# Opening of an attention and SwiGLU kernel: order of transposes, scores, sums and casts

## Chip, core and metric

The kernel runs on one core of one Trainium2 chip. The metric is the device time of one execution in microseconds (us). The engines are TensorE (PE; its weight loads are listed as PEld), VectorE (DVE), ScalarE (ACT), GpSimd (POOL) and SyncE (SP), which only issues transfers here.

## What is computed

Causal attention with a window of 64 positions, for 8 batches and 8 heads of 576 positions with 64 values each, and then a SwiGLU block on the 4608 rows of 512 values that come out of it.

```python
scores = q @ k.T / sqrt(64)
mask = (rel >= 0) & (rel < 64)        # rel = row - column
attn = softmax(where(mask, scores, -1e9))
x = (attn @ v).transpose(0, 2, 1, 3).reshape(4608, 512)
g = x @ w_gate
out = (g * sigmoid(g) * (x @ w_val)) @ w_out     # d_ff = 1536
```

## The kernel before

The rows are worked on in nine tiles of 512 (`t` = 0 to 8). A tile is one batch's first 512 positions, except for tile 7, which holds the last 64 positions of all batches. Within a tile `u` = 0 to 3 counts pairs of heads. The order of instructions on each engine is the order in which the program issues them (a manual schedule); waits between engines come from the tiles and their buffers.

For each pair, `scores` (L200) multiplies keys and queries block by block into `s_ps`, a pair of PSUM banks, and ACT takes the exponential into `E`. Tile 0 has its mask as a bias that is added in PSUM by four matmuls with the identity (L227); later tiles multiply with a mask on DVE. `sums` (L242) adds up the weights with a matmul against ones (`d_ps`), and ACT forms the inverse as a logarithm (L251) and an exponential of its negative (L253). `values` (L257) multiplies weights and values into `ao_ps`, and DVE multiplies by the inverse into `xT` (L269). `gate_value` (L294) makes one of 12 steps `m` of the gate: four matmuls into `g_ps`, four into `v_ps`, then Silu on ACT and a product on DVE (`gate_end`). `project` (L331) has 12 chunks per output block of 128 rows.

Tile 0 is the opening. Its q and k come as float32 over SP and ACT, are cast by ACT, DVE and POOL (`casts`, L402), and turned by PE transposes into `tp` (L173), from which DVE or ACT copies q (L410) and DVE copies k (`split_k`, L176). The loop at L403 does this for one pair, then its scores. `keep_warm` (L358) issues matmuls whose result nobody reads. v of batch 0 comes as float32 over SP, is cast by POOL (`cast_v`, L146), and a copy shifted by half a block is made by DVE (`shift_v`, L150). For `values` all four blocks of both copies are needed.

The weights come over POOL's queue, which casts them: gate and value weights in column blocks of 256 (`weights_gv`, L158), then q of batch 1 (`load_qk`), then the output weights in three blocks (`weights_o`, L164), then v of batch 1. A ring allows eight of POOL's transfers to be open; the ninth waits for the first to land. The first two gate steps are built up pair by pair (`gate_part`, L275) between the values of the pairs.

The keys of batch 1 are loaded by ACT in steps m = 0 to 3, and in m = 4 to 7 each pair is cast by ACT, transposed by PE and copied by DVE within the same step (L456 to L461). From m = 8 on DVE turns the queries of batch 1 (`turn_q`). Then come the scores of tile 1 with halves of tile 0's projection between them (L467 to L470).

PSUM has two pools with two buffers per name: `ps_a` holds wide pairs of banks (scores, sums, values, and `tp` of batch 1), `ps_f` single banks under "g" and "v" (gate, projection, sums, `tp` of batch 0, warm-up).

Of the kernel before, what the change touches and what calls it, by code (L numbers as in the profile page):

```python
# [8 lines left out]
P = 128  # L9
FP32 = mybir.dt.float32  # L10
BF16 = mybir.dt.bfloat16
AF = mybir.ActivationFunctionType
# [5 lines left out]
def kernel(  # L18
# [127 lines left out]
    def cast_v(t, which=range(4)):  # L146
        for i in which:
            nc.gpsimd.tensor_copy(v1[t % 2][:, i], staged[t, "v"][:, i])  # L148

    def shift_v(t, copy, lo=0, hi=4):  # L150

        a, b = v1[t % 2], v2[t % 2]
        top = min(hi, 3)
        if top > lo:
            copy(b[64:128, lo + 1:top + 1], a[64:128, lo:top])
        copy(b[0:64, lo:hi], a[0:64, lo:hi])

    def weights_gv(f0, f1):  # L158
        for src, dst in ((moe_w_gate, wg), (moe_w_val, wv)):
            nc.gpsimd.dma_start(  # L160
                dst[:, :, f0:f1], src[:, f0:f1].rearrange("(c r) f -> r c f", r=P)
            )

    def weights_o(c0, c1):  # L164
        nc.gpsimd.dma_start(
            wo[:, c0:c1, :],
            moe_w_out[P * c0:P * c1].rearrange("(c r) f -> r c f", r=P),
        )
# [31 lines left out]
    def scores(t, u):  # L200

        qT = queries[t][:, u, :]
        E = epool.tile([P, 2, 512], BF16, name="E", tag="E")
        s_ps = ps_a.tile([P, 2, 512], FP32, name="s_ps", tag="a")
        if t == LAST:
            pieces = [
                (c, b, b + 1, kT[t % 2 if b < 4 else 2], P * (b % 4) + 64 * c)
                for b in range(8) for c in range(2)
            ]
        else:  # L210
            pieces = [(1, 0, 1, None, 0)] + [
                (j % 2, j, min(8, j + 2), kT[t % 2], 64 * j) for j in range(8)
            ]
        for i, (c, lo, hi, src, x) in enumerate(pieces):
            for h in range(2):
                r = slice(64 * h, 64 * h + 64)
                nc.tensor.matmul(  # L217
                    blocks(s_ps[64 * c:64 * c + 64, h], t, lo, hi),
                    zero[r] if src is None else src[r, u, x:x + 64],
                    blocks(qT[r], t, lo, hi),  # L220
                    start=t >= TURNED or i < 2, stop=t >= TURNED,
                )
        if t < TURNED:
            for c in range(2):
                for h in range(2):
                    r = slice(64 * h, 64 * h + 64)
                    nc.tensor.matmul(  # L227
                        s_ps[64 * c:64 * c + 64, h], identb[r, r],
                        bias[r, c ^ h].rearrange("r e i c x -> r (e i c x)"),
                        start=False, stop=True,  # L230
                    )
        nc.scalar.activation(E[:], s_ps[:], AF.Exp, scale=0.125)  # L232
        if t >= TURNED:
            nc.vector.tensor_mul(  # L234
                E[:].rearrange("r h x -> r (h x)"),
                E[:].rearrange("r h x -> r (h x)"),
                maskl[:].rearrange("r h e b x -> r (h e b x)") if t == LAST
                else mask[:].rearrange("r h e i c x -> r (h e i c x)"),
            )
        weights[t, u] = E  # L240

    def sums(t, us, d_ps, apart=False):  # L242

        for i, u in enumerate(us):
            for h in range(2):
                nc.tensor.matmul(  # L246
                    d_ps[64 * h:64 * h + 64, i], ones[:, 0:D], weights[t, u][:, h, :]
                )
        n = len(us)
        r = fsb.tile([P, 2, 512], FP32, name="r", tag="r", bufs=4)  # L250
        nc.scalar.activation(r[:, 0:n], d_ps[:], AF.Ln)  # L251
        for x in [r[:, i:i + 1] for i in range(n)] if apart else [r[:, 0:n]]:
            nc.scalar.activation(x, x, AF.Exp, scale=-1.0)  # L253
        for i, u in enumerate(us):
            inverse[t, u] = r[:, i]

    def values(t, u, o_ps):  # L257
        E = weights.pop((t, u))
# [10 lines left out]
        nc.vector.tensor_mul(xT[t][:, u, :], o_ps[:], inverse.pop((t, u)))  # L269

    def products(t, u):
        sums(t, (u,), ps_f.tile([P, 1, 512], FP32, name="d_ps", tag="v"))
        values(t, u, ps_a.tile([P, 2, 512], FP32, name="ao_ps", tag="a")[:, 0])

    def gate_part(t, ms, tiles, c):  # L275
        for m, pair in zip(ms, tiles):
            for ps, w in zip(pair, (wg, wv)):
                nc.tensor.matmul(  # L278
                    ps[:], w[:, c, P * m:P * m + P], xT[t][:, c, :],
                    start=(c == 0), stop=(c == 3),  # L280
                )
# [76 lines left out]
    def keep_warm(n):  # L358
        for _ in range(n):
            nc.tensor.matmul(warm[0:D], ones[:, 0:D], ones[:])  # L360

    keep_warm(8)
    nc.gpsimd.memset(tri[:], 1.0)
    for a in range(2):
        half = tri[64 * a:64 * a + 64]
# [30 lines left out]
    def wide(name):  # L396
        return ps_a.tile([P, 2, 512], FP32, name=name, tag="a")

    def join(copy, dst, src):
        copy(dst.rearrange("r e (h d) -> r h e d", h=2), src)  # L400

    casts = ((on_a, on_v), (on_p, on_v), (on_p, on_p), (on_p, on_p))  # L402
    for u in range(4):  # L403
        hs = slice(2 * u, 2 * u + 2)
        tps = []
        for i in range(2):
            join(casts[u][i], first[:, i, u], raw[i][:, hs])
            tps.append(ps_f.tile([P, 512], BF16, name="tp", tag="gv"[i]))
            transposes(tps[i], first[:, i, u])
        (on_v if u else on_a)(queries[0][:, u, :], tps[0][:])  # L410
        split_k(kT[0][:, u, :], tps[1][:])
        keep_warm(1)
        if u == 3:
            sums(0, (0, 1), wide("d_ps"))
        scores(0, u)
    weights_gv(0, 256)
    for i in range(0, 4, 2):
        cast_v(0, (i, i + 1))
        shift_v(0, on_v, i, i + 2)
    weights_gv(256, 512)  # L420
    weights_gv(512, 768)
    for f in range(768, DFF, 256):
        weights_gv(f, f + 256)
    load_qk(1)
    weights_o(0, 4)
    weights_o(4, 8)
    weights_o(8, 12)
    load_v(nc.gpsimd, v1[1], 1)
    keep_warm(4)
    sums(0, (2, 3), wide("d_ps"), apart=True)  # L430
    keep_warm(4)
    pairs = [gate_tiles() for _ in range(2)]
    for u in range(0, 4, 2):
        o_ps = wide("ao_ps")
        for i in range(2):
            values(0, u + i, o_ps[:, i])
        for c in range(u, u + 2):
            gate_part(0, (0, 1), pairs, c)
    set_silu()
    raw_k = stage.tile([P, H, 4, D], FP32, name="k_f", tag="k")  # L440
    for m in range(12):
        if m < 2:
            gate_end(0, m, pairs[m])
        else:
            gate_value(0, m)
        if m == 2:
            for i in range(4):
                nc.vector.tensor_copy(
                    mask[:, 0, :, i], tri[:].rearrange("r c (x e) -> r e c x", e=16)
                )  # L450
            nc.vector.memset(mask[64:128, 0, :, 0, 0, :], 0.0)
            nc.vector.tensor_copy(mask[:, 1], mask[:, 0])
        if m < 4:
            hs = slice(2 * m, 2 * m + 2)
            load_runs(nc.scalar, raw_k[:, hs], k, 1, hs)
        elif m < 8:  # L456
            u = m - 4
            tp = ps_a.tile([P, 512], BF16, name="tp", tag="a")
            join(on_a, keys[:, u], raw_k[:, 2 * u:2 * u + 2])
            transposes(tp, keys[:, u])  # L460
            split_k(kT[1][:, u, :], tp[:])  # L461
        if m >= 8:
            turn_q(1, m - 8)
# [12 lines left out]
        shift_v(1, on_v, i, i + 1)  # L476

    def d_tile():
        return ps_f.tile([P, 1, 512], FP32, name="d_ps", tag="v")

    for u in range(2):
        sums(1, (u,), d_tile())
    project(0, 2)
    for u in range(4):
        if u > 1:
            sums(1, (u,), d_tile())
        values(1, u, wide("ao_ps")[:, 0])
    project(0, 3)

    for t in range(1, NT):  # L490
# [68 lines left out]
```

## Time and profile before

| | |
|---|---|
| Median of three runs | 340.98 us (340.88 to 341.24) |
| Profiled run | 342.31 us, of which the span covers 340.4 |
| Granted TensorE clock, mean | 0.997 |
| First matmul of the gate's step m=2 | 24.54 us |
| First projection matmul of tile 0 | 46.78 us |
| First gate matmul of tile 1 | 61.10 us |

A line of the profile's timeline gives start, duration, engine, source line, operation, and what it writes and reads; `x4` means four instructions merged, and the bracket at its end the idle time of the engine before it and what ended it. A line of the waits gives who waited for whom, the total, how often, and the longest. In the page's 40 slices a digit is the busy share in tenths. The rates of a DMA view count bytes as they arrive, so a transfer that casts float32 to bfloat16 reads twice as many.

### The profile page before, as it was taken

The numbers are of one execution on the slowest core, as the hardware profiler recorded it, in microseconds if no ns is written. First come the engines' busy times: TensorE is split into PE (matmuls) and PEld (weight loads), VectorE is DVE, ScalarE is ACT, GpSimd is POOL, SyncE is SP. The second block draws the span as 40 slices with busy tenths as digits, with TensorE's granted clock in tenths as the row PEclk, the third lists the DMA queues.
The fourth block names the chain that finished last, engine by engine and source line by source line (L and its number), as shares of the span: only waits on it lengthen the run. The fifth ranks groups of instructions, "written<-read, shape, count | busy, mean of one in ns | idle before, by whom it ended". The sixth has DMA issues, their size and how long they took to land.

```text
span 340.4 us, 6984 instructions
## 1 busy us (share of the span) xinstructions
PE 327.5 (96%) x2732; PEld 154.3 (45%) x2732; DVE 214.8 (63%) x318; ACT 167.8 (49%) x237; POOL 140.2 (41%) x252
## 2 busy tenths in 40 slices
PE   8777899999999999999999999999999999999994
PEld 3443344444544444444444444454445444454441
DVE  5545568378766775696578657865777576754431
ACT  3654466435653566346534753376337633673310
POOL 4963536846756976206521997065200000000000
PEclk9999999999999999999999999999999999999998
DMA  8999999999699679809960999499501220020013
GB/s 261 207 180 239 213 188 225 136 210 196 116 228 228 73 120 235 178 4 160 212 155 2 138 181 184 31 135 210 134 0 33 75 73 2 16 79 32 3 31 92
DMA packets 84113, 44.38 MB, mean 130 GB/s; under 512 B 63856, under 2 KB 78704, under 8 KB 84080
## 3 DMA queue, kind: packets, MB, share of 16 engines
q0 software_dynamic: 48304, 22.30, 53.2%
q1 hardware_dynamic: 33760, 19.54, 21.1%
q10 hardware_dynamic: 2016, 2.10, 2.2%
q8 instruction: 21, 0.34, 0.4%
q14 instruction: 12, 0.10, 0.1%
HBM read 54.00 MB, written 9.44 MB: 186 GB/s over the span
## 4 chain that ended last, share of the span: by engine, by line
PE 90%; DMA 5%; DVE 2%; ACT 1%; issue 0%; DVEq 0%
PE o_ps L307 26%; PE g_ps L298 26%; PE v_ps L298 26%; PE s_ps L217 3%; DMA k_f<-in_k_dram 3%; PE ao_ps L263 3%; PE d_ps L246 3%; PE warm L360 2%; PE tp L173 1%; DVE xT L269 1%; PE g_ps L278 1%; DMA out_dram<-os__4430 1%; DMA out_dram<-os__4392 1%; DMA out_dram<-os__4411 1%; PE v_ps L278 1%; DVE kT L176 0%
## 5 line engine op out<-in xcount | busy, mean ns | idle before, releaser
L291 ACT ACTIVATE sg<-g_ps 128x512 f32<-128x512 f32 x108 | 64.4, 597 | 120.1 <-PE g_ps L298 88.2
L292 DVE TENSOR_TENSOR hT<-sg,v_ps 128x512 bf16<-128x512 f32 x108 | 74.8, 694 | 62.4 <-PE v_ps L298 61.3
L298 PE MATMUL g_ps<-xT,wg 128*128 128x512 bf16 x424 | 108.8, 379 | 0.0
L298 PE MATMUL v_ps<-xT,wv 128*128 128x512 bf16 x424 | 108.8, 379 | 0.0
L307 PE MATMUL o_ps<-wo,hT 128*128 128x512 bf16 x432 | 99.0, 380 | 0.0
L107 POOL DMA_DIRECT2D k_s<-in_k_dram x112 | 60.4, 545 | 28.5 <-DMA q_s<-in_q_dram 20.4
L298 PEld LDWEIGHTS <-wv 128*128 128x128 bf16 x424 | 41.5, 98 | 50.1
L298 PEld LDWEIGHTS <-wg 128*128 128x128 bf16 x424 | 41.3, 98 | 49.3 <-issue 0.3
L307 PEld LDWEIGHTS <-hT 128*128 128x128 bf16 x432 | 39.7, 98 | 45.5 <-issue 0.4
L269 DVE TENSOR_TENSOR xT<-ao_ps,r 128x512 bf16<-128x512 f32 x36 | 24.8, 691 | 25.5 <-ACT r L253 20.3
L232 ACT ACTIVATE E<-s_ps 128x1024 bf16<-128x1024 f32 x36 | 35.1, 1021 | 9.1 <-PE s_ps L217 5.5
L195 DVE STREAM_TRANSPOSE kT<-k_s 128x512 bf16<-128x512 bf16 x28 | 35.9, 1283 | 0.0
L251 ACT ACTIVATE r<-d_ps 128x512 f32<-128x512 f32 (+1 forms) x34 | 20.9, 614 | 22.2 <-PE d_ps L246 22.2
L234 DVE TENSOR_TENSOR E<-E,mask 128x1024 bf16<-128x1024 bf16 x28 | 20.9, 754 | 10.4 <-ACT E L232 10.3
L87 POOL DMA_DIRECT2D q_s<-in_q_dram x28 | 15.2, 549 | 29.1 <-DVE qT L185 17.8
L148 POOL CAST v<-v_f 128x512 bf16<-128x512 f32 x24 | 15.2, 651 | 21.4 <-DMA v_f<-in_v_dram 15.0
L253 ACT ACTIVATE r<-r 128x512 f32<-128x512 f32 (+1 forms) x35 | 22.4, 642 | 1.1
L185 DVE STREAM_TRANSPOSE qT<-q_s 128x512 bf16<-128x512 bf16 x32 | 22.5, 705 | 0.0
L263 PE MATMUL ao_ps<-E,v 128*64 128x64 bf16 x576 | 15.7, 196 | 2.3 <-DVE xT L269 2.3
L263 PEld LDWEIGHTS <-v 128*64 128x64 bf16 x576 | 14.0, 112 | 6.9 <-issue 3.4
L246 PE MATMUL d_ps<-E,ones 128*64 128x512 bf16 x72 | 14.5, 391 | 1.2 <-ACT E L232 1.2
L217 PE MATMUL s_ps<-qT,kT 64*64 64x128 bf16 (+1 forms) x640 | 12.4, 213 | 0.8 <-DVE kT L176 0.8
(93 smaller groups left out, 176.9 us busy)
## 6 DMA issues: line engine op xcount, KB each, us to landing
q_s<-in_q_dram POOLq DMA_DIRECT2D x28, 248.0 KB, 6.9
k_s<-in_k_dram POOLq DMA_DIRECT2D x112, 56.0 KB, 4.9
v_f<-in_v_dram SPq DMA_DIRECT2D x24, 256.0 KB
v<-in_v_dram POOLq DMA_DIRECT2D x16, 128.0 KB, 5.2
k_f<-in_k_dram ACTq DMA_DIRECT2D x6, 256.0 KB
wg<-in_moe_w_gate_dram POOLq DMA_DIRECT2D x6, 256.0 KB, 7.2
wv<-in_moe_w_val_dram POOLq DMA_DIRECT2D x6, 256.0 KB, 7.7
wo<-in_moe_w_out_dram POOLq DMA_DIRECT2D x3, 512.0 KB, 15.0
```

Of the source, the lines that this page charges most:

```text
L107: nc.gpsimd.dma_start(k_s[p0:p0 + 32, g, :, 0:w], k[b, a:H:2, s:s + P].rearrange("u (r e) d -> r u (e d)", e=4) [:, :, 32 * c:32 * c + w],)
L185: nc.vector.transpose(queries[t][:, u, :].rearrange("r (e x) -> r e x", e=16), staged[t][0][:, u].rearrange("r (e d) -> r e d", d=D)[:, :, ...
L195: nc.vector.transpose(dst[:, u, :].rearrange("r (g x e) -> r g e x", g=4, e=4), k_s[:, :, u].rearrange("r g (e d) -> r g e d", d=D)[:, :, ...
L217: nc.tensor.matmul(blocks(s_ps[64 * c:64 * c + 64, h], t, lo, hi), zero[r] if src is None else src[r, u, x:x + 64], blocks(qT[r], t, lo, h ...
L232: nc.scalar.activation(E[:], s_ps[:], AF.Exp, scale=0.125)
L246: nc.tensor.matmul(d_ps[64 * h:64 * h + 64, i], ones[:, 0:D], weights[t, u][:, h, :])
L263: nc.tensor.matmul(blocks(o_ps[64 * h:64 * h + 64], t, m, m + 1), (v1, v2)[m // 4][t % 2][:, m % 4, 2 * u + h, :] if t == LAST else (v2, v ...
L269: nc.vector.tensor_mul(xT[t][:, u, :], o_ps[:], inverse.pop((t, u)))
L291: nc.scalar.activation(sg[:], g_ps[:], AF.Silu)
L292: nc.vector.tensor_mul(hT[t][:, m, :], sg[:], v_ps[:])
L298: nc.tensor.matmul(ps[:], w[:, c, P * m:P * m + P], xT[t][:, c, :], start=(c == 0), stop=(c == 3),)
L307: nc.tensor.matmul(o_ps[:], hT[t][:, c, P * s:P * s + P], wo[:, c, :], start=(c == 0), stop=(c == 11),)
```

## The change

In tile 0's scores the bias matmuls come first (they open the accumulation) and the blocks of keys follow. The transposes of a pair and their copies become a function `turn_pe(u)`, and the order of the opening is written out: transposes of pair u+1 stand before the scores of pair u. For the first two pairs the logarithm of the sums comes before the scores of pair 3, and the inverse after them. The sums of pairs 2 and 3 go to single banks of `ps_f`, as two logarithms and then two inverses. Values of each pair get a buffer of their own, and the gate's parts of a pair come after the values of the next. Warm-up matmuls are 7, 3 x 1 and 3, where they were 8, 4 x 1, 4 and 4. Of v, blocks 0 and 1 are cast by POOL before its first weight transfer, and 2 and 3 by DVE. The weight columns 768 to 1280 come in one transfer each instead of two, and q of batch 1 is loaded before the last weight columns. The key casts of batch 1 move from steps m = 4 to 7 to m = 6 to 9, and the transposes to m = 7 to 10, a step after their cast.

```diff
@@ scores @@
-        for i, (c, lo, hi, src, x) in enumerate(pieces):
-            ...
-                    start=t >= TURNED or i < 2, stop=t >= TURNED,
         if t < TURNED:
             ...
-                        start=False, stop=True,
+                        start=True, stop=False,
+        for c, lo, hi, src, x in pieces:
+            ...
+                    start=t >= TURNED, stop=t >= TURNED or (lo > 5 and src is not None),
@@ opening @@
-    keep_warm(8)
+    keep_warm(7)
...
-    for u in range(4):
+    def turn_pe(u):
...
-        keep_warm(1)
-        if u == 3:
-            sums(0, (0, 1), wide("d_ps"))
-        scores(0, u)
+    turn_pe(0)
+    keep_warm(1)
+    scores(0, 0)
+    turn_pe(1)
+    keep_warm(1)
+    turn_pe(2)
+    scores(0, 1)
+    keep_warm(1)
+    turn_pe(3)
+    scores(0, 2)
+    cast_v(0, (0, 1))
     weights_gv(0, 256)
-    for i in range(0, 4, 2):
-        cast_v(0, (i, i + 1))
-        shift_v(0, on_v, i, i + 2)
+    d_ps, r = wide("d_ps"), room(2)
+    for u in range(2):
+        totals(0, u, d_ps[:, u])
+        inverse[0, u] = r[:, u]
+    log(r, d_ps[:])
+    scores(0, 3)
+    invert(r)
+    for i in range(4):
+        if i > 1:
+            on_v(v1[0][:, i], staged[0, "v"][:, i])
+        if i % 2:
+            shift_v(0, on_v, i - 1, i + 1)
     weights_gv(256, 512)
     weights_gv(512, 768)
-    for f in range(768, DFF, 256):
-        weights_gv(f, f + 256)
+    weights_gv(768, 1280)
     load_qk(1)
+    weights_gv(1280, 1536)
...
-    keep_warm(4)
-    sums(0, (2, 3), wide("d_ps"), apart=True)
-    keep_warm(4)
+    keep_warm(3)
+    for u in (2, 3):
+        d_ps = ps_f.tile([P, 512], FP32, name="d_ps", tag="gv"[u % 2])
+        totals(0, u, d_ps[:])
+        inverse[0, u] = room(1)[:, 0]
+        log(inverse[0, u], d_ps[:])
+    for u in (2, 3):
+        invert(inverse[0, u])
     pairs = [gate_tiles() for _ in range(2)]
-    for u in range(0, 4, 2):
-        o_ps = wide("ao_ps")
-        for i in range(2):
-            values(0, u + i, o_ps[:, i])
-        for c in range(u, u + 2):
-            gate_part(0, (0, 1), pairs, c)
+    for u in range(4):
+        values(0, u, one("ao_ps"))
+        if u:
+            gate_part(0, (0, 1), pairs, u - 1)
+    gate_part(0, (0, 1), pairs, 3)
@@ gate of tile 0, step m @@
-        elif m < 8:
-            u = m - 4
+        if 6 <= m < 10:
+            u = m - 6
+            join(on_a, keys[:, u], raw_k[:, 2 * u:2 * u + 2])
+        if 7 <= m < 11:
+            u = m - 7
             tp = ps_a.tile([P, 512], BF16, name="tp", tag="a")
-            join(on_a, keys[:, u], raw_k[:, 2 * u:2 * u + 2])
             transposes(tp, keys[:, u])
             split_k(kT[1][:, u, :], tp[:])
```

`totals`, `room`, `log` and `invert` are the parts of the former `sums`.

More of the change, by code (lines that the diff above doesn't have):

```diff
@@ L213, in scores @@
             ]
-        for i, (c, lo, hi, src, x) in enumerate(pieces):
[L215 to L220, printed above, removed]
-                    start=t >= TURNED or i < 2, stop=t >= TURNED,
-                )
         if t < TURNED:
@@ L229, in scores @@
                         bias[r, c ^ h].rearrange("r e i c x -> r (e i c x)"),
-                        start=False, stop=True,
+                        start=True, stop=False,
                     )
+        for c, lo, hi, src, x in pieces:
+            for h in range(2):
+                r = slice(64 * h, 64 * h + 64)
+                nc.tensor.matmul(
+                    blocks(s_ps[64 * c:64 * c + 64, h], t, lo, hi),
+                    zero[r] if src is None else src[r, u, x:x + 64],
+                    blocks(qT[r], t, lo, hi),
+                    start=t >= TURNED, stop=t >= TURNED or (lo > 5 and src is not None),
+                )
         nc.scalar.activation(E[:], s_ps[:], AF.Exp, scale=0.125)
@@ L240, in scores, with totals, room, log @@
         weights[t, u] = E
[L242 to L255, printed above, removed]
+    def totals(t, u, d_ps):
+        for h in range(2):
+            nc.tensor.matmul(
+                d_ps[64 * h:64 * h + 64], ones[:, 0:D], weights[t, u][:, h, :]
+            )
+    def room(n):
+        return fsb.tile([P, 2, 512], FP32, name="r", tag="r", bufs=4)[:, 0:n]
+    def log(r, d_ps):
+        nc.scalar.activation(r, d_ps, AF.Ln)
+    def invert(r):
+        nc.scalar.activation(r, r, AF.Exp, scale=-1.0)
+    def sums(t, u, d_ps):
+        totals(t, u, d_ps)
+        r = room(1)[:, 0]
+        log(r, d_ps)
+        invert(r)
+        inverse[t, u] = r
     def values(t, u, o_ps):
@@ L271, in products @@
     def products(t, u):
-        sums(t, (u,), ps_f.tile([P, 1, 512], FP32, name="d_ps", tag="v"))
+        sums(t, u, ps_f.tile([P, 512], FP32, name="d_ps", tag="v")[:])
         values(t, u, ps_a.tile([P, 2, 512], FP32, name="ao_ps", tag="a")[:, 0])
@@ L400, in join, with one @@
         copy(dst.rearrange("r e (h d) -> r h e d", h=2), src)
+    def one(name):
+        return ps_a.tile([P, 2, 512], FP32, name=name, tag="a")[:, 0]
     casts = ((on_a, on_v), (on_p, on_v), (on_p, on_p), (on_p, on_p))
-    for u in range(4):
+    def turn_pe(u):
         hs = slice(2 * u, 2 * u + 2)
@@ L411 @@
         split_k(kT[0][:, u, :], tps[1][:])
-        keep_warm(1)
-        if u == 3:
-            sums(0, (0, 1), wide("d_ps"))
-        scores(0, u)
-    weights_gv(0, 256)
-    for i in range(0, 4, 2):
-        cast_v(0, (i, i + 1))
-        shift_v(0, on_v, i, i + 2)
+    turn_pe(0)
[9 more added lines that the diff above has]
+    cast_v(0, (0, 1))
+    weights_gv(0, 256)
+    d_ps, r = wide("d_ps"), room(2)
[4 more added lines that the diff above has]
+    scores(0, 3)
+    invert(r)
+    for i in range(4):
[3 more added lines that the diff above has]
+            shift_v(0, on_v, i - 1, i + 1)
     weights_gv(256, 512)
     weights_gv(512, 768)
-    for f in range(768, DFF, 256):
-        weights_gv(f, f + 256)
+    weights_gv(768, 1280)
     load_qk(1)
+    weights_gv(1280, 1536)
     weights_o(0, 4)
@@ L478, in d_tile @@
     def d_tile():
-        return ps_f.tile([P, 1, 512], FP32, name="d_ps", tag="v")
+        return ps_f.tile([P, 512], FP32, name="d_ps", tag="v")[:]
     for u in range(2):
-        sums(1, (u,), d_tile())
+        sums(1, u, d_tile())
     project(0, 2)
@@ L485 @@
         if u > 1:
-            sums(1, (u,), d_tile())
-        values(1, u, wide("ao_ps")[:, 0])
+            sums(1, u, d_tile())
+        values(1, u, one("ao_ps"))
     project(0, 3)
```

## The prediction

> **What bounds the kernel now.** I read the page first, then the waits of the first 60 us, then the timeline there and the landings of the transfers.
>
> ```profile
> span 340.4 us, 6984 instructions
> PE 327.5 (96%) x2732; PEld 154.3 (45%) x2732; DVE 214.8 (63%) x318; ACT 167.8 (49%) x237; POOL 140.2 (41%) x252
> ...
> PE   8777899999999999999999999999999999999994
> ...
> DMA  8999999999699679809960999499501220020013
> ```
>
> TensorE (PE) is the bound from the sixth slice (8.5 us each) to the end; a gain can come only from the first five. There the DMA engines are full too, which decides below how much of a gain is kept. The waits of 0 to 60 us (total, times, longest):
>
> ```profile
> PE tp L173 <- ACT k_b L400: 2.7, 4, 1.4
> ...
> PE ao_ps L263 <- DVE xT L269: 2.3, 3, 0.9
> ...
> PE d_ps L246 <- ACT E L232: 1.2, 1, 1.2
> ...
> PE s_ps L217 <- DVE kT L176: 0.8, 2, 0.4
> ```
>
> These four sum to 7.0 us, and the change addresses all of them. The timeline shows their cause (start, duration, engine, line; in brackets the idle time before):
>
> ```profile
> 13.23 1.02 ACT L251 ACTIVATE r<-d_ps 128x1024 f32<-128x1024 f32 x1 [0.28 <-PE d_ps L246]
> ...
> 14.28 1.06 ACT L253 ACTIVATE r<-r 128x1024 f32<-128x1024 f32 x1
> ...
> 15.24 1.01 ACT L232 ACTIVATE E<-s_ps 128x1024 bf16<-128x1024 f32 x1
> ...
> 17.80 1.15 ACT L253 ACTIVATE r<-r 128x512 f32<-128x512 f32 x2
> 17.91 0.69 DVE L269 TENSOR_TENSOR xT<-ao_ps,r 128x512 bf16<-128x512 f32 x1 [2.43 <-PE ao_ps L263]
> ...
> 24.54 1.02 PE L298 MATMUL g_ps<-xT,wg 128*128 128x512 bf16 x4
> ...
> 31.26 0.40 PE L173 MATMUL tp<-identb,k_b 128*128 128x128 bf16 x4 [1.38 <-ACT k_b L400]
> ```
>
> ScalarE (ACT) runs the last exponential (15.24) behind logarithm and inverse of the first pair. The first full gate step (m=2) begins at 24.54. Its steps take 8 matmuls x 0.216 = 1.73 us, but m=4 to m=8 begin at 27.99, 31.49, 33.95, 36.58, 39.19, since the transposes behind each wait for a cast of the same step.
>
> The last transfers before the second batch are read from POOL, whose next issues waited for the three blocks of wo:
>
> ```profile
> 42.03 0.55 POOL L87 DMA_DIRECT2D q_s<-in_q_dram x1 [1.65 <-DMA wo<-in_moe_w_out_dram]
> ...
> 44.55 0.54 POOL L87 DMA_DIRECT2D q_s<-in_q_dram x1 [1.97 <-DMA wo<-in_moe_w_out_dram]
> ...
> 47.09 0.54 POOL L87 DMA_DIRECT2D q_s<-in_q_dram x1 [2.00 <-DMA wo<-in_moe_w_out_dram]
> ```
>
> Issue plus time to landing agrees: 27.20+14.5, 28.87+15.4, 31.82+15.0 give 41.7, 44.3, 46.8. The second half of the projection starts at 50.07; after four matmuls, at 51.0, it needs the third block. So that block has 4.2 us to spare, no more.
>
> [...] from 27 to 38 us the q0 and ACT queues together take 120% of the 16 engines' time (over 100% since packets overlap). [...] Here issues beside DVE copies (13.44 to 14.90) took 0.74 to 0.89 us, those with DVE idle (15.78 to 17.24) 0.75 to 0.77[...]. [...] Here PE's longest wait after the start is 1.38 us and the granted clock from 4 us on is 1.00[...]. [...] the four bias matmuls take 0.40 us together, where one of 512 columns alone takes 0.38.
>
> **The change part by part.** Times are of the profiled span (340.4; that run was 342.3, the three timed ones 340.88 to 341.24; I carry the difference in us over to 340.98).
>
> *First transposes and bias.* One warm matmul less (0.43 each at the slow clock) lets the transposes start when their ACT cast ends, 4.75 instead of 5.08: 0.28. The bias now runs while PE waits for the kT copy; before, 0.24 stood behind the scores. First exponential at about 7.3 instead of 7.79.
>
> *Transposes a pair ahead.* The k transposes all use one PSUM buffer (the warm-up holds the other of that tag): in the built program those of pair 2 wait for DVE's copy of pair 1. So the order is copy (0.68), transposes (0.43 until read), copy. Stepping through: second exponential 9.75 (was 9.85, nothing gained), third 11.1 (was 11.92).
>
> *Logarithm, scores, inverse.* ACT now runs exponential 3 (11.1), logarithm (12.1), exponential 4 (13.2; was 15.24: 2.0 gained), inverse (14.2 to 15.3). The sums of pair 3 then follow at 14.3 (was 16.30), two logarithms and two inverses of 0.6 each end at 17.7 (was 18.95). xT of the first pair starts at 15.3 (was 17.91).
>
> *v casts.* Two of four move from POOL to DVE; a POOL cast takes 0.62, a DVE one 0.43 to 0.67 by the rows of L400. With shifts of 0.49, 0.62, 0.60, 0.42, DVE is done at about 14.7, before PE wants v. But the two left on POOL now stand before the first weight issue, and they wait for v, which landed at 9.7 and 10.6 by the trace's completion events. First weight issue: 9.39 becomes 11.3. A first landing comes 4.2 (second wg) to 5.0 us (first) after issue: wg at 15.5 to 16.3, wv one transfer (1.4) later, 17.0 to 17.7. The first gate part has xT at 16.0 and waits for wv.
>
> *Values in separate banks.* They remove 0.87 and 0.86 of idle: values of the next pair no longer wait for the xT read of the last. From wv at 17.0 to 17.7 PE has left: three matmuls 0.65, values 0.44, part 0.86, values 0.44, xT 0.85, two parts 1.7 (the first beside the xT). Step m=2 begins at 21.3 to 22.0, say 21.7 (was 24.54): 2.8 gained.
>
> *Key casts early.* ACT casts at m=6 to 9, PE transposes a step later. The four steps took 39.19-27.99 = 11.20; undisturbed they take 4 x 1.73 + 4 x 0.25 (transposes) = 7.92: 3.3 gained. ACT per step: 0.60+0.62 = 1.22 of 1.73, hidden. DVE per step at m=8 to 10: 0.69+0.69+0.70 = 2.08 against 1.98 of PE, 0.3 behind in all, hidden by the second buffer. Sum without transfers: 6.1.
>
> *The transfers.* Bytes are unchanged, so where PE catches up with the stream the stream decides. Lag: it starts 1.9 later, but before, the POOL casts behind the first pair of issues left a thin stretch (slices of 82 and 51 GB/s near 15 us). Over 12 to 20 us the mean is 168 GB/s, over 20 to 26 it is 188: 8 x 20/188 = 0.85 us of full rate are missing, which closes, since issues are now back to back. Merging 768:1280 doubles the row length: I take up to 0.6 off, an estimate from 188 GB/s at 20 to 26 us (rows of 256 columns) against 202 at 38 to 46 (longer rows): 7% of the 8 us or so in which four such blocks pass. 1.9-0.85-0.6 is 0.4. Bounds -0.5 and +1.9; I take +0.4. The four q transfers now precede the last weights (1280:1536), so those land where q did (25.83+13.4 = 39.2), at 39.6. Step m=10 needs their wv half before 43.51; undisturbed PE would be there at 21.7 + 8 x 1.73 + 3 x 0.25 + 0.86 = 37.2, so it waits 2.4. The third wo block lands at 47.2 for a need at 51.0. Both caps allow the same: 43.5-39.6 = 3.9 and 51.0-47.2 = 3.8. Behind them v of batch 1 (landed by 50.2) precedes its shifts (about 50.1 to 52.2), and the DVE turns of batch 2, at 70.6 before, need keys landed at 63.8: 6.8 to spare. So 3.9 is kept: **340.98 - 3.9 = 337.1**.
>
> **The rivals.**
> (a) PE, not the stream, decides: all 6.1 kept, 334.9. For it: the lag may be nil and the merged rows faster. Against: 4.2 us to spare at the third wo block.
> (b) The late first weights are not made up: lag 1.9, so 4.2-1.9 = 2.3 kept, 338.7. For it: 97% of the engines' time is q0's in the first 60 us. Against: the thin stretch.
> (c) The edits at the head don't do what they say, because the k transposes stand in one buffer and the wv wait grows; only the key casts count: 3.3, 337.7.
> (d) Slower: [...] For it: fewer warm-up matmuls, 13 for 20. [...]
>
> **How the numbers follow.** The stream-bound case 0.50, (a) 0.15, (b) 0.20, (c) 0.07, (d) 0.08. Its own range is lag -0.3 to +1.2, 336.4 to 337.9; (a) and (b) at 334.9 and 338.7 are taken in: 334.8 to 339.0. Faster by over 0.2% (0.7 us, about what a measurement tells from no change) 0.91, within 0.02, slower 0.07[...].
>
> **What would show it.** Right: step m=2 at 21.3 to 22.0; fourth exponential near 13.2; no PE wait for k_b; a new PE wait for weights at m=10 of about 2 us; the third wo block landing near 47.2 and used at once. Wrong: m=10 undisturbed (a), m=2 later than 23 (c), clock digits below 9 (d), the third block at 48.5 or later (b).

## The result and the profile after

The changed kernel takes 339.35 us (median of four runs, 338.55 to 339.43) against 341.07 (340.88 to 341.24) in the same sitting: ratio 0.9944, 95% interval 0.9927 to 0.9962. It is faster by 1.7 us by the medians (1.9 by the ratio), where 3.9 were forecast. Run again on another chip it was 339.50 against 341.45, ratio 0.9942 [0.9926, 0.9958]. A run more than 1.5% above the fastest of its kernel counts as slow and is left out; here these are two runs of experiment e3.

The page of the profile after, its lines that answer to those shown of before:

```profile
span 337.7 us, 6970 instructions
...
PE 325.9 (97%) x2725; PEld 153.7 (46%) x2725; DVE 214.4 (63%) x320; ACT 167.3 (50%) x238; POOL 138.8 (41%) x248
...
PE   7699899999999999999999999999999999999994
...
PEclk9979999999999999999999999999999999999998
...
DMA  7999999999999579929950999299501320020013
```

TensorE is full from the third slice on but for one 8 (it was from the sixth). But the third clock digit is a 7: there PE is busy at a reduced clock. The DMA digits show the engines as full as before. The waits of 0 to 60 us (total, times, longest):

```profile
POOL q_s L87 <- DMA wo<-in_moe_w_out_dram: 5.7, 3, 2.0
...
PE ao_ps L270 <- DVE v L156: 1.8, 1, 1.8
DVE v L445 <- DMA v_f<-in_v_dram: 1.6, 1, 1.6
...
PE g_ps L305 <- DMA wg<-in_moe_w_gate_dram: 1.0, 1, 1.0
```

None of the four PE waits of before is left among the larger ones. In their place PE waits once for v, which waits for its transfer, and at step m=10 for gate weights (1.0 us for wg, then 0.3 for wv). The timeline (start, duration, engine, line; idle time before it in brackets):

```profile
12.78 1.03 ACT L232 ACTIVATE E<-s_ps 128x1024 bf16<-128x1024 f32 x1
...
14.59 0.47 DVE L445 CAST v<-v_f 128x512 bf16<-128x512 f32 x1 [1.57 <-DMA v_f<-in_v_dram]
...
15.58 1.18 ACT L255 ACTIVATE r<-r 128x512 f32<-128x512 f32 x2
...
16.18 0.57 PE L270 MATMUL ao_ps<-E,v 128*64 128x64 bf16 x24 [1.79 <-DVE v L156]
16.61 1.29 DVE L276 TENSOR_TENSOR xT<-ao_ps,r 128x512 bf16<-128x512 f32 x2 [0.49 <-PE ao_ps L270]
...
19.33 0.63 PE L285 MATMUL v_ps<-xT,wv 128*128 128x512 bf16 x1
...
19.75 0.63 PE L285 MATMUL g_ps<-xT,wg 128*128 128x512 bf16 x1
...
39.20 1.04 PE L305 MATMUL g_ps<-xT,wg 128*128 128x512 bf16 x4 [1.00 <-DMA wg<-in_moe_w_gate_dram]
...
40.53 1.04 PE L305 MATMUL v_ps<-xT,wv 128*128 128x512 bf16 x4 [0.30 <-DMA wv<-in_moe_w_val_dram]
...
48.40 0.55 POOL L87 DMA_DIRECT2D q_s<-in_q_dram  x1 [1.96 <-DMA wo<-in_moe_w_out_dram]
```

ScalarE's work ends earlier, as meant: the fourth exponential starts at 12.78 (was 15.24), and the last inverse ends at 15.58 + 1.18 = 16.76 (was 18.95). Then 512-column matmuls follow each other by 0.42 (19.33, 19.75), where they did by 0.216: from 18.38 to 21.79 us the granted clock is 0.50. At m=10 (39.20) PE stands for weights. The third block of wo has landed when POOL goes on (48.40 in the last line, 48.1 by the completion events); PE, whose second half of the projection began at 47.33, comes to it at about 48.2. The chain of waits names the transfers as what lies before that (start, us, what; the last wv is POOL's fourteenth transfer and was issued at 23.82, when the sixth had landed at 23.53; in this trace and the first of before each of POOL's transfers from the ninth to the 34th was issued 0.28 us or more after the one eight ahead of it had landed):

```profile
15.52 8.01 DMA wv<-in_moe_w_val_dram
23.53 0.28 issue
23.82 16.67 DMA wv<-in_moe_w_val_dram
40.49 0.05 issue
40.53 1.04 PE v_ps L305 x4
```

**One number orders all traces.** In all fourteen traces of this study the run's time less the start of tile 1's first gate step lies between 281.02 and 281.25 us. What comes after that point differs by no more than 0.23 us; the opening decides. So this table, of one profiled run each, can be read as a table of times (landings from the transfers' completion events, us):

| kernel | last wv landed | third wo landed | tile 1 starts | less last wv | less third wo | profiled run |
|---|---|---|---|---|---|---|
| before | 34.5 | 46.8 | 61.10 | 26.62 | 14.30 | 342.31 |
| before, again | 35.2 | 47.7 | 59.21 | 23.97 | 11.50 | 340.44 |
| after | 40.5 | 48.1 | 58.36 | 17.88 | 10.25 | 339.41 |
| after, again | 40.2 | 48.8 | 59.04 | 18.80 | 10.19 | 340.10 |
| e1 weights first | 38.1 | 45.8 | 56.02 | 17.87 | 10.23 | 337.04 |
| e1 again | 38.4 | 47.1 | 57.29 | 18.93 | 10.20 | 338.31 |
| e2 keys alone | 36.0 | 48.5 | 59.42 | 23.39 | 10.94 | 340.65 |
| e3 head alone | 40.5 | 48.1 | 62.16 | 21.69 | 14.07 | 343.21 |
| e4 warm | 39.2 | 47.1 | 57.34 | 18.16 | 10.20 | 338.38 |
| e5 weights later | 41.4 | 49.1 | 59.29 | 17.87 | 10.23 | 340.44 |
| e6 keys and queue | 40.9 | 48.6 | 58.82 | 17.87 | 10.23 | 340.07 |
| e7 first and warm | 38.9 | 46.5 | 56.75 | 17.88 | 10.25 | 337.79 |
| e8 weights earlier | 38.2 | 45.8 | 59.52 | 21.37 | 13.74 | 340.56 |
| e9 q last | 34.1 | 46.6 | 57.09 | 23.00 | 10.51 | 338.11 |

No tile 1 starts sooner than 17.87 us after the last gate weights, or sooner than 10.19 after the third block of wo. Where 17.87 or 17.88 stands, PE waited for gate weights and found the third block landed 0.03 to 0.06 us before it was needed; where 10.19 or 10.20 stands, the third block came last. The two caps lie so close because the block follows the last wv in the same queue, by 7.6 us in these five traces, and PE's work between the two takes 7.7.

### The profile page after: what moved, and what is told of

The parts are those of the page before. It is cut to its first block, busy times and chain, and to the rows that moved or that the text cites. A ratio compares the mean times of both kernels' runs of the same rounds, so it can differ in the third digit from the quotient of the medians.

```text
span 337.7 us, 6970 instructions
## 1 busy us (share of the span) xinstructions
PE 325.9 (97%) x2725; PEld 153.7 (46%) x2725; DVE 214.4 (63%) x320; ACT 167.3 (50%) x238; POOL 138.8 (41%) x248
## 4 chain that ended last, share of the span: by engine, by line
PE 84%; DMA 12%; POOL 1%; DVE 1%; issue 0%; SPq 0%
PE o_ps L314 26%; PE v_ps L305 25%; PE g_ps L305 25%; DMA wv<-in_moe_w_val_dram 7%; PE s_ps L226 3%; PE d_ps L244 3%; PE ao_ps L270 3%; DMA v_f<-in_v_dram 2%; DMA k_f<-in_k_dram 1%; POOL wg L160 1%; DMA out_dram<-os__4407 1%; DMA out_dram<-os__4426 1%; DMA out_dram<-os__4388 1%; POOL wv L160 0%; DVE os__4388 L321 0%; DVE os__4407 L321 0%
## 5 line engine op out<-in xcount | busy, mean ns | idle before, releaser
L87 POOL DMA_DIRECT2D q_s<-in_q_dram x28 | 15.3, 556 | 24.3 <-DVE qT L185 14.5
L94 POOL DMA_DIRECT2D q_s<-in_q_dram x16 | 8.6, 618 | 9.7 <-DVE qT L185 9.7
```

## The experiments

The theory of the prediction, called the stream theory: the start of tile 1 hangs on the queue that POOL feeds. Its rival after the result: PE's own path (the half clock, the wait for v) ate the gain. A third question came from the number itself: was the first profile of before a fair one?

**Before, unchanged, profiled again.**

> The kernel before, unchanged, for a second trace. Its profiled run was 342.31 us, 1.2 over the median of its timed runs, while that of the changed kernel lay on its median. Theory A (the first profile was not typical, so the waits read from it were too long): the span is near 339.3, and the steps m=4 to m=8 of tile 0 take about 10.0 us instead of 11.20. Theory B (the profile was typical and only the time around the span differed): span 340.4, the steps take 11.2 again.

341.17 us, ratio 0.9999 [0.9990, 1.0008]. The waits and the timeline of this second trace:

```profile
PE tp L173 <- ACT k_b L400: 1.7, 4, 0.7
```

```profile
48.00 0.55 POOL L87 DMA_DIRECT2D q_s<-in_q_dram  x1 [2.00 <-DMA wo<-in_moe_w_out_dram]
...
48.18 0.60 PE L307 MATMUL o_ps<-wo,hT 128*128 128x512 bf16 x2
```

The first profile was not typical, as theory A had it: the wait for the key casts is 1.7, not 2.7; m=4 to m=8 take 10.24 us, not 11.20. The last keys landed at 33.6, where the first trace had 38.3, and the third wo block at 47.7 instead of 46.8: in the first trace POOL's queue had moved more by 40 us (4.60 MB against 4.42) and ACT's queue, which loads the keys, less by 32 us (1.21 against 1.40). Another 0.9 us was lost in the first trace before any of this. Its record of a full clock begins at 7.35 us, that of the second trace at 4.37, and the first eight transposes took 1.03 us, not 0.62, so that the first exponential began at 7.79 and not at 6.86. So in the first trace PE was later and the stream earlier than here. The second half of the projection begins at 48.18, and its fifth matmul, which needs the third block, at 49.05: 1.3 us to spare, against the 4.2 that the prediction read. The first profiled run, 342.31, lies 1.2 over the median of before; this one 0.7 under.

**The first weights ahead of the v casts on POOL (after otherwise).**

```diff
-    cast_v(0, (0, 1))
     weights_gv(0, 256)
+    cast_v(0, (0, 1))
```

> The changed kernel, but POOL issues the first two weight transfers ahead of its two casts of v. Stream theory (the weights' stream begins 1.7 us late behind those casts, and step m=10 of the gate and the third block of wo wait for it): first issue at about 9.9 instead of 11.57, the weights 1280:1536 land at about 38.8 instead of 40.49, the third wo block at 46.4 instead of 48.11, tile 1's first gate step at about 56.7 instead of 58.36, time 337.6 (the changed kernel 339.35). Rival (what was lost is TensorE's own time, half clock from 18.4 to 21.7 us and step m=2 at 23.47 instead of 21.7): no change beyond 0.4 us, 339.3, or somewhat slower, since v is ready later.

338.34 us, ratio 0.9912 [0.9891, 0.9934] (runs 337.04 to 339.15). First issue 9.5 instead of 11.6, last gate weights 38.1 instead of 40.5, third wo block 45.8 instead of 48.1, tile 1 at 56.02. This profiled run is the fastest of the six, and the time is 0.7 over the 337.6 of the stream theory. Its waits show that PE still stood for weights at m=10:

```profile
PE g_ps L305 <- DMA wg<-in_moe_w_gate_dram: 0.7, 1, 0.7
```

Run again on a third chip:

> The version with the first two weight transfers ahead of the two v casts again, beside the next three on one chip: ratio to before near 0.9912, about 338.4, last gate weights at about 38.1 us.

338.01 us, 0.9902 [0.9880, 0.9924]. Two swapped lines are worth 1.1 to 1.4 us more than the change alone (by the ratios to before, on different chips), and PE still stands for the stream: the direction is that of the stream theory, the size somewhat less. In the second trace PE waited at m=10 too (0.7 and 0.3), and then 0.8 for the third block of wo.

**The key casts alone (before otherwise).**

```diff
-        elif m < 8:
-            u = m - 4
+        if 6 <= m < 10:
+            u = m - 6
+            join(on_a, keys[:, u], raw_k[:, 2 * u:2 * u + 2])
+        if 7 <= m < 11:
+            u = m - 7
             tp = ps_a.tile([P, 512], BF16, name="tp", tag="a")
-            join(on_a, keys[:, u], raw_k[:, 2 * u:2 * u + 2])
```

> The kernel before with one part of the change alone: key casts at m=6 to 9, transposes a step later. Stream theory: the weights keep their old order and land by 34.5, the third wo block at 46.8, just ahead of the new need at about 47.7; the steps m=4 to m=8 run undisturbed (7.9 instead of 11.2 us), gain 3.3 from the profile's waits, 337.8, or 2.1 and 339.0 if the profile of before overstated them by 1.2. Then this part alone is worth as much as the whole change. Rival (the parts add): it is worth what the whole change has less the 1.1 us by which step m=2 begins earlier, that is 0.6, 340.5.

340.61 us, ratio 0.9990 [0.9978, 1.0001]: nothing that can be told. PE did gain: m=11 began at 40.52, where the two traces of before have 44.37 and 42.49. But its waits name a new one:

```profile
DVE qT L185 <- DMA q_s<-in_q_dram: 3.1, 1, 3.1
...
PE s_ps L217 <- DVE kT L176: 1.8, 3, 1.0
...
PE v_ps L298 <- DVE hT L292: 0.8, 1, 0.8
```

q of batch 1, still behind all weights here, landed at 40.9. DVE stood 3.1 us for it, with the hT products and key copies queued behind, for which PE then waited. The time is that of the rival (340.5), but neither theory's reason fits: PE lost the gain again while DVE stood for q. The third block of wo, at 48.5, would have allowed tile 1 at 58.7, only 0.7 sooner than it began. That q ahead of the last weights lets the casts pay is tried below, in e6.

**The head alone (after with the key casts back in steps 4 to 7).**

```diff
-        if 6 <= m < 10:
-            ...
-        if 7 <= m < 11:
-            u = m - 7
+        elif m < 8:
+            u = m - 4
             tp = ps_a.tile([P, 512], BF16, name="tp", tag="a")
+            join(on_a, keys[:, u], raw_k[:, 2 * u:2 * u + 2])
```

> The changed kernel with its key casts and transposes put back to m=4 to 7, so the head of the change alone. Stream theory: the keys of batch 1 land at about 38 whatever the head does, the transposes of the last pair stand before step m=8, which can't begin before about 39 (39.19 before); the 1.1 us gained at m=2 are waited away there: 340.7 to 341.1, no gain. Rival (the parts add): 1.1 gained, 340.0.

342.14 us (median of twelve runs), ratio 1.0006 [0.9983, 1.0028], with a wide spread (339.4 to 343.8). That is slower than either theory had said. The chain of its profiled run (start, us, what):

```profile
24.91 11.96 DMA k_f<-in_k_dram
36.87 0.02 issue
36.89 0.63 ACT k_b L407
37.52 0.05 issue
37.56 0.40 PE tp L173 x4
```

It reached m=4 at 27.29, between the traces of before (27.99 and 27.07), and then waited for keys that landed from 30.5 to 38.4: m=8 only at 40.25. As timed, the head without the later casts gives nothing, and the parts do not add: by the ratios 0.3 us for the casts and -0.2 for the head (neither told from nothing), against 1.9 to 2.0 for the whole.

A rival was left untested here. The clock fell to half twice in this trace (17.6 to 21.0 and 31.2 to 34.6 us; the mean is 0.75 over 18 to 24 and 0.89 over 24 to 40 us), and over its twelve runs the time follows the mean granted clock: 339.4 and 339.6 us at 0.999, 342.1 to 343.2 at 0.990 to 0.992. The line through them rises by 1.1 us for each us of clock time lost (one minus the mean granted clock, times the run's time). So the head may be worth about as much as the whole change where the clock holds. Long waits for keys and a fallen clock come together (PE waited 2.21 us for a key cast until 31.18, and four matmuls from 31.57 took 1.91 us, where they took 1.03 from 27.29), so this is a fit and not a trial; no run held this kernel's clock up.

**After again, beside the next three.**

> The changed kernel unchanged, beside the next three on one chip. Stream theory: the first gate step of tile 1 follows the landing of the weights 1280:1536 by about 17.9 us (58.36 after 40.49 in its first trace), and the run ends about 281.1 us after that step begins (as in all six traces so far): ratio to before near 0.9944, and where the clock is or isn't halved between 18 and 24 us in this trace makes no difference to that. Clock theory: a trace with an undisturbed clock there would show tile 1 some 1.5 us earlier.

339.50 us (338.46 to 340.10). The same gain, with another last wait in its trace; the third block of wo landed at 48.8:

```profile
PE o_ps L314 <- DMA wo<-in_moe_w_out_dram: 0.8, 1, 0.8
```

**Eight warm-up matmuls more (after otherwise), put where PE waits for v.**

```diff
         invert(inverse[0, u])
+    keep_warm(8)
     pairs = [gate_tiles() for _ in range(2)]
```

> The changed kernel with eight more warm-up matmuls between the sums of pair 3 and the values, 8 x 0.216 = 1.7 us in the 1.8 us in which TensorE waited for v there. Clock theory (the half clock from 18.4 to 21.7 us cost the time): the clock stays at 1.00, step m=2 begins at about 21.8 instead of 23.47, tile 1 1.7 us earlier, 337.7. Stream theory: clock and m=2 as above, but the wait for weights at m=10 grows by as much, the weights land at 40.5 as before and tile 1 begins at 58.4: same time as the changed kernel, within 0.4 us.

339.07 us, ratio 0.9936 [0.9923, 0.9949]. Windows of after, then of this kernel: stretch, length, busy time (and count) of PE, PEld, DVE, ACT, POOL, clock, DMA share, GB/s:

```profile
14.40:17.80 3.40, 1.01 (x26) 0.67 (x27) 2.66 (x5) 3.38 (x6) 3.40 (x5) 1.00 1.36 172
18.40:21.70 3.30, 3.30 (x38) 1.52 (x38) 0.90 (x2) 0.00 (x0) 1.71 (x4) 0.50 1.39 184
18.00:24.00 6.00, 5.96 (x49) 2.59 (x48) 1.93 (x3) 1.15 (x3) 3.05 (x6) 0.72 1.36 191
```

```profile
14.40:17.80 3.40, 2.37 (x41) 1.35 (x40) 2.08 (x4) 3.38 (x6) 3.40 (x6) 1.00 1.41 186
...
18.00:24.00 6.00, 5.96 (x56) 2.66 (x55) 2.67 (x4) 1.68 (x3) 3.19 (x6) 1.00 1.38 200
```

The clock stayed whole (1.00 in both stretches), and m=2 began at 22.19 instead of 23.47 and 24.82. The time is 0.4 below that of after on the same chip, with intervals that overlap: PE came earlier to m=10 and waited there all the same (0.9 us). In the ten timed runs of after the time hardly follows the clock either (339.19 at 0.999, 338.46 and 338.55 at 0.995 and 0.994). So the half clock cost after little or nothing: the rival falls, as long as the stream is this late.

**The first weights later still: three v casts on POOL ahead of them.**

```diff
-    cast_v(0, (0, 1))
+    cast_v(0, (0, 1, 2))
...
-        if i > 1:
+        if i > 2:
```

> The changed kernel with three instead of two v casts on POOL ahead of the first weights (and one instead of two on VectorE). The third v block lands at about 11.9, so the first weight issue moves from 11.57 to about 12.5, and v is ready on VectorE no later than before. Stream theory: all landings and the time 0.9 us later than the changed kernel, 340.3. Rival (TensorE's path decides): not slower, or faster by up to 0.4 with less work on VectorE.

339.91 us, ratio 0.9959 [0.9943, 0.9975]: 0.4 slower than after on this chip, half of what the stream theory said, and the intervals overlap. First issue 12.5, last gate weights 41.4, third wo block 49.1, tile 1 at 59.29. The landings moved by 0.9 and 1.0 against the first trace of after, by 1.2 and 0.2 against the second. In all four traces with the transfers of after (both of after, e3, e4) both landed earlier than here. The direction is shown, the size is not settled.

**Key casts and the queue's order, without the new head (before otherwise).**

```diff
-    for f in range(768, DFF, 256):
-        weights_gv(f, f + 256)
+    weights_gv(768, 1280)
     load_qk(1)
+    weights_gv(1280, 1536)
```

with the key casts of the second experiment.

> The kernel before with two parts of the change: key casts at m=6 to 9, and POOL's queue in the new order (weights 768:1280 in one transfer, q of batch 1 ahead of the weights 1280:1536). The rewritten head is left out: first weight issue at 9.5, step m=2 at about 24. The key casts alone gave 0.1%, as q of batch 1 landed at 40.9 and VectorE stood still 3.1 us for it. Stream theory: these two parts carry the gain: q lands by 37, the weights 1280:1536 at about 40.0, TensorE is there at 39.3, tile 1 at about 57.9, 339.0, as fast as the whole change. Rival (the head's earlier m=2 is what carries the gain): 340.3 or more.

340.13 us, ratio 0.9959 [0.9945, 0.9974]: 1.3 us of the 2.0 that the whole gave on this chip, with the old opening. The stream theory had said 339.0, the rival 340.3 or more, so the size speaks for neither. The first gate step (m=2) began at 23.60, as before, and PE waited 0.8 us for wg at m=10. Over the casts alone (e2) it gains 1.1 us by the ratios, and the intervals lie apart: so the queue's new order does let the casts pay, though the merged transfer came with it. The rewritten head is left with some 0.6 us, which the intervals do not tell from nothing; it reaches the same caps. The new order without the later casts was not run.

**The best version: weights first, and five warm-up matmuls ahead of the values.**

```diff
-    cast_v(0, (0, 1))
     weights_gv(0, 256)
+    cast_v(0, (0, 1))
...
+    keep_warm(5)
     pairs = [gate_tiles() for _ in range(2)]
```

> The version with the weights first, and five more warm-up matmuls ahead of the values (5 x 0.216 = 1.1 us in the 1.0 us in which TensorE waited for v). Stream theory: same time as without them, within 0.4 us, as the wait for weights at m=10 remains. Clock theory: its runs spread from 337.0 to 339.2 because the clock falls in some; held up, all lie near 337.2.

337.79 us, ratio 0.9894 [0.9880, 0.9909], runs 337.42 to 338.39. It beats both kernels: its interval lies below those of after (from 0.9926). Over the first swap alone, on the same chip, it gains 0.2 us, which the intervals do not tell apart; its runs lie closer together. In the three traces with the weights first (e1 twice and this) the last gate weights landed at 38.1 to 38.9, in the four with the transfers of after at 39.2 to 40.5.

**The first weights earlier still: the last pair's casts moved from POOL to ACT and DVE.**

```diff
-    casts = ((on_a, on_v), (on_p, on_v), (on_p, on_p), (on_p, on_p))
+    casts = ((on_a, on_v), (on_p, on_v), (on_p, on_p), (None, on_v))
...
     turn_pe(2)
+    weights_gv(0, 256)
+    join(on_a, first[:, 0, 3], raw[0][:, 6:8])
     scores(0, 1)
...
     cast_v(0, (0, 1))
-    weights_gv(0, 256)
```

with the five warm-up matmuls.

> The version with the weights first and the warm-up, and in addition the casts of the last pair moved off POOL (q to ACT between two exponentials, k to VectorE), so that POOL issues the first weights about 1.1 us earlier, at 8.4. Stream theory: landings 0.5 to 1.1 us earlier (v of batch 0 shares the engines at that time and may land later), last gate weights at about 37.3, time 0.5 to 1.0 us below the version without it, 337.6. Rival (the engines were full with v already, so the earlier issue moves nothing): same time, v later by as much as the weights are earlier.

339.64 us, ratio 0.9954 [0.9935, 0.9973]: slower than e7, which neither theory expected. Its waits and a window:

```profile
DVE v L447 <- DMA v_f<-in_v_dram: 4.1, 1, 4.1
...
PE ao_ps L270 <- DVE v L156: 2.5, 1, 2.5
```

```profile
18.00:24.00 6.00, 5.43 (x62) 2.56 (x64) 2.06 (x4) 0.25 (x1) 2.58 (x4) 0.50 1.33 203
```

The weights, issued at 8.2, are now under way beside v (DMA share 1.33 over 10 to 18 us, 1.27 in e7): v's last block lands at 16.85 instead of 14.12 in e7. PE waits 2.5 for it, falls to half clock (0.50 over 18 to 24 us) and begins m=2 at 26.36. The gate weights are as early as in the first trace of e1 (38.2), the third wo block too (45.8), and tile 1 begins 13.7 after it: now PE's path is the cap. How much of it is the clock? Two of the thirteen runs had a mean granted clock of 0.998 and took 337.61 and 338.12, as e7 does; the four at 0.990 took 340.5 to 341.6, and the line through all rises by 1.0 us for each us of clock time lost. So the late v seems to cost mainly by way of the clock; as in e3 this is a fit. Both theories were incomplete; there are two sides, and e1 and e7 lie between them.

**q of batch 1 after the last weights (e1 otherwise), its turns two each at m=10 and 11.**

```diff
     weights_gv(768, 1280)
-    load_qk(1)
     weights_gv(1280, 1536)
+    load_qk(1)
...
-        if m >= 8:
-            turn_q(1, m - 8)
+        if m >= 10:
+            for u in range(2 * m - 20, 2 * m - 18):
+                turn_q(1, u)
```

> The version with the weights first, but q of batch 1 behind the last gate weights again, and its turns on VectorE two each in steps 10 and 11, so that q may land at 38 us. It takes away the wait for weights at m=10 (1.0 us in the trace) alone. If two limits of the stream lie at the same time, as predicted (gate weights at m=10 and the third wo block in the projection), the time stays within 0.4 us, and a wait for wo takes its place. If only the gate weights limit, 1.0 us is gained: 337.4.

338.55 us, ratio 0.9927 [0.9901, 0.9952]; no gain over e1 on the same chip (338.01). The wait at m=10 is gone, the weights being there at 34.1, and nothing is won, because the third block of wo (46.6) would allow a start at 56.8 and PE's own path gives 57.09. In this trace its clock had fallen (0.80 over 18 to 24 us), so the wait for wo that I looked for in place of the other does not show.

## Why the prediction went wrong, point by point

**Right: what bounds.** PE catches up with the stream and stands for weights at m=10, 1.3 us where about 2 was said; the third block of wo is used when it lands. No wait for the keys of batch 1 is left on PE. "Both caps allow the same" holds: in after, e1, e5, e6 and e7 the gate weights came last and the third block within 0.06 us of them, in e4 and the second traces of after and e1 it was the third block. Clearing one (e9) gains nothing.

**Right: ScalarE's chain.** Fourth exponential 12.8 (13.2 said), end of the inverses 16.8 (17.7), first weights issued at 11.6 (11.3), landed 16.2 and 17.6 (15.5 to 16.3 and 17.0 to 17.7). In the second trace wv landed at 18.9, and PE waited 1.8 us for it.

**Wrong, the larger part: "I carry the difference in us over to 340.98".** This is the step that failed: the slack of one trace was spent as a saving on any run. In its own span the prediction's sum says 342.31 - 3.9 = 338.4. The profiled run of after was 339.41, a miss of 1.0. The other 1.3 came from subtracting the same 3.9 from the timed 340.98. But the 3.9 was the slack of PE against the stream in one trace, and a cap is a time of its own: how late PE was before does not move it. In the first trace PE was 1.9 us later at tile 1 than in the second, 0.9 by the first exponential (7.79 for 6.86, with the record of the full clock from 7.35 for 4.37) and 1.0 at the key casts, and that lateness is part of the 3.9. (The 1.00 that the prediction read "from 4 us on" covers what was recorded, from 7.35.) With the third block at the predicted 47.2, the table's 10.2 and 281.1 for the rest of the run, the same reasoning gives 47.2 + 10.2 + 281.1 = 338.5. The slack of 4.2 itself was rightly read from its trace, and was 1.3 in the next.

**Not settled, the smaller part: the third block "at 47.2".** It landed 0.9 later, at 48.1, in the profiled run of after. The 47.2 was 46.8 of one trace and the lag of "+0.4". By the two traces of each kernel the lag was 1.2 (48.1 and 48.8 against 46.8 and 47.7). But e2 has the transfers of before, with the block at 48.5, and e3 and e4 those of after, with 48.1 and 47.1. By these three and four the means are 47.7 and 48.0, a lag of 0.4 as forecast, and then it was the 46.8 that was early. The spread within one set of transfers is 1.7, so the traces do not tell which. They do tell that the lag was not made up of the parts that the sum had, so that its 0.4 would be luck. POOL's queue began with a hole; this is its row in the DMA view of 11 to 14 us, before and then after (packets, MB, share):

```profile
q0 software_dynamic: 678, 0.34, 89.4%
```

```profile
q0 software_dynamic: 99, 0.05, 18.0%
```

In the mean of the three and the four traces the queue with the transfers of after was 0.24 MB behind at 14 us, level at 24 (1.90 against 1.89 MB) and 0.06 MB ahead at 40. So the whole late start was made up by 24 us, where the prediction gave 0.85 of 1.9 for it; and from 24 to 40 us, where the merged rows pass, there came 0.05 MB more, at the 205 GB/s of 40 to 44 us some 0.2 us and not 0.6. The other way went something that was not in the sum at all: when the third wo block was complete, the queue had moved 5.97 to 6.09 MB in the four traces, against 5.93 in each of the three. Some 0.1 MB of other transfers, 0.5 us, went ahead of its last bytes. Which these were is not shown; v of batch 1 is next in the queue.

With the third block 0.9 later than the 47.2 that the prediction had, as in the first trace of after, 338.5 becomes 339.4: the time measured. The same with middle values, as an estimate: before's 341.07 puts tile 1 at 59.9, the mean landing of 47.7 allows 57.9, and the 2.0 between them less a lag of 0.4 leaves 1.6 us; 1.7 were measured.

**Wrong without effect: "Step m=2 begins at 21.3 to 22.0".** It was 23.47 and 24.82. DVE was to be done with v at 14.7; v's last block landed at 14.57, not at 12.83 as in the trace of before (13.71 in its second), and PE waited 1.8 us for it. Then the clock was halved (0.50 from 18.38 to 21.79 us). The mark set for rival (c), "m=2 later than 23", was met, by another cause than its buffer; in e4, with m=2 at 22.19, the time was 0.4 less, which the intervals do not tell from nothing.

**Wrong: the key casts' 3.3 as a term of its own.** It is PE time, and PE did gain it in e2 (m=4 to the start of m=11 in 12.98 us, against 16.38 and 15.42 in the traces of before: 3.4 and 2.4); but the time did not move. The sum of 6.1 for PE alone was never tested, since PE met the stream first in the changed kernel.

**The rivals.** (b), late weights not made up, came nearest in size (2.3 kept, 338.7), though the bytes were made up; its mark, the third block at 48.5 or later, was met in the second trace and not in the first. (d)'s size was my estimate of what a fallen clock costs, which no trace of before showed. Its mark, clock digits below 9, was met once, by 3.4 us at 0.50 that came behind the wait for v and not for weights; with the clock held up (e4) the time was 0.4 less, which the intervals do not tell from nothing. (a) would need the wo block by about 334.9 - 281.1 - 10.2 = 43.6; the earliest seen is 45.8.

## What to carry to other kernels

Where a saturated queue sets when a stage can end, work out the time from the landing itself (landing + what must follow), not as a saving taken off a total: PE's lateness in one profile is not a gain that adds, and a slack should be read from more than one trace before it is spent. Cost every edit of an opening first by what it does to that queue's first issue and to the order of what follows in it; here two swapped lines on POOL gave 1.1 to 1.4 us, and the rewritten head, on top of casts and queue, some 0.6. Then look for the other side: issuing still earlier starved v (its last block at 16.85 us instead of 14.12), and the gain went back (339.64 instead of 337.79). And where runs of one kernel spread, set their times against their granted clocks before judging a part: e3 and e8 look different then.

## What the runs showed of the hardware that I had not expected

The clock was halved though PE had stood no longer than 1.79 us at a time: in after it was 0.50 from 18.38 to 21.79 us, and in the 3.41 us before that PE was busy for 1.59. Seven traces over the same two stretches:

| kernel | PE busy, 14.4 to 17.8 us | clock, 18.4 to 21.7 us |
|---|---|---|
| after | 1.01 | 0.50 |
| after, again | 1.09 | 0.71 |
| e8 weights earlier | 1.24 | 0.50 |
| e9 q last | 1.30 | 0.70 |
| e1 weights first | 1.86 | 1.00 |
| before | 2.22 | 1.00 |
| e4 warm | 2.37 | 1.00 |

In e9 the fall had begun within the first stretch (0.87 there). So in these seven the clock fell where PE had been busy for 1.30 us or less of the 3.40 and held where it had been for 1.86 or more; what it goes by they do not show. The one trial of it is e4, which added eight matmuls to after. The ends of matmuls are modelled and some records missing, so the last digit is not to be trusted.

Two traces of one kernel differed at the start of tile 1 by 1.9 us (before), 1.3 (e1) and 0.7 (after). In before it was PE that came later, by 0.9 us at the first exponential and 1.0 at the casts of the keys; in e1 the third block of wo landed 1.3 later although the last gate weights were only 0.2 later, with 6.07 MB moved by POOL's queue by then instead of 5.89. Why the engines divide themselves differently from run to run is not settled.
